# Attention and a mixture of experts on one core: the last attention step reordered, and expert 0's second weights loaded and split later

## The chip, the cores and the metric

The kernel runs on 1 core of one Trainium2 chip. The metric is the device time of one execution in microseconds (us). A core has TensorE (PE, with its weight loads shown as PEld), VectorE (DVE), ScalarE (ACT), GpSimd (POOL) and SyncE (SP, which here only issues loads and stores). Each engine works through its own instructions in order; semaphores tie the engines together.

## The reference

Inputs are q, k, v of shape 8 x 8 x 576 x 64 (batch, head, token, width), a gain vector g, and the experts' weights: a gate 512 x 8, a local gate 512 x 1, w1 8 x 512 x 1024 and w2 8 x 1024 x 512, all float32.

```python
kv = einsum('bhsd,bhse->bhde', k, v)
x = einsum('bhsd,bhde->bhse', q, kv)
x = x / sqrt(mean(x * x, -1) + 1e-6) * g
...
logits = x @ w_gate
local = sigmoid(x @ w_local)
...
e = argmax(logits) if s == 0 or local < 0.5 else previous e
out = softmax(logits)[e] * (relu(x @ w1[e]) @ w2[e])
```

Heads are laid side by side, so x is 8 x 576 x 512 for the second half. Each token goes to one expert; which one depends, where the local gate is high, on the token before it in its batch.

## The kernel before, in words

**Attention in 16 steps.** The batches are taken in four groups of two, and each group in four steps of two heads: step i is group i // 4, head pair i % 4 (`NST` = 16). For a step, SyncE loads six tiles of 288 KB: kt and vt of two batches (`load_kv`, two steps ahead of their product) and qt of two batches (`load_q`). TensorE makes k times v (`kv`, L375), turns kv and multiplies it with the gate for the logits (`turn_kv` L409, `logits_of` L425), turns q (`turn_q` L439 and, for its last columns, `turn_last` L417), and multiplies q with kv in two parts (`q_kv`, L460). GpSimd copies kv into the block-diagonal tile kvz (`kvb_of`, L399), ScalarE copies the logits' columns beside it (L429) and the results out of PSUM into raw (L464). Squares are taken on GpSimd or ScalarE (`squares`, L495 and L493) and summed on VectorE (`sums`, L500).

**Order by letters.** For PE, ACT, DVE and POOL the program's order is the engine's order (`manual_schedule`). In the loop over i, each letter of `STEP` (or of `LATE[i]` for the last steps) calls one branch of `work_of` (L859). Those of interest here: `Q`, `c`/`R` and `a` are q times kv of step i (products of the first part; products and copy of the second part; copy of the first part). `0` and `1` are the two kv copies of step i+1 on GpSimd. `T` and `U` are the turns of q of step i+1, `L` and `l` the logits of step i+1 and their copy into kvz. `m`, `p`, `q`, `b` push on the routing of an earlier group (`SLOTS`, `adv`). `G` closes the pool of kt and vt and issues two gathers on GpSimd (L770), the rows of the first two blocks of 128 tokens of expert 0 (xa). `2` and `3` scale such a block on VectorE (L808) and copy its gate on GpSimd (L928); `4` and `5` turn it on TensorE (L820), cast it on ScalarE (L824) and subtract on VectorE (L825). `o` stores up to three chunks of finished rows to DRAM and, in the steps of `LOADED`, loads one weight piece; `e` loads q of step i+3.

**Weights.** An expert has eight pieces of 512 KB: 0 to 3 of w1, 4 to 7 of w2. `wload` loads a piece into one of four buffers (wst). `wsplit` makes two float32r tiles of it: hi is a copy on ScalarE (L230 or L233), lo the subtraction wst - hi (L231 or L234), by default on VectorE. In the loop `w` is the copy and `v` the subtraction, in the steps of `SPLIT`. Expert 0's piece 7 is split behind the loop, with its subtraction on GpSimd (L1136). Every load and store of SyncE goes through `fetch` (L184), one queue in program order; up to the last step each waits for the landing of the sixth one before it (`LANES`).

**Routing.** `rows_out` (norms, logits, keys) and `route` (each token's place in its expert's list) are generators, pushed on by `adv`. In `route` VectorE builds one-hot tiles co, ab and lo (L710, L717, L740: place columns and lanes compared with a counter, 16-bit results), and TensorE multiplies lo with ab (L723), nine small products, whose sums are the lists of tokens.

**The first expert.** `first_wide` computes relu(w1 x) of the first two blocks, in four pairs of 128 of the 1024 hidden columns (24 products of 256 columns each, L961, L966, L967); behind each pair ScalarE and VectorE make hh and hl (L1031, L1032), and hooks run: a0, a2, a4, a6 of `PASS`. In a hook, `2` and `3` push on the routing of the current group by two or three stages, `o` stores, `s` takes the last step's sums and starts the last group. At a0 to a4 that is the routing of the third group, whose products L723 are in a4 on TensorE, ahead of the fourth pair. Then `second` multiplies with w2 for the first block (hooks b) and the second (hooks c), and scatters the rows from GpSimd (L997); the third and fourth blocks and the other seven experts follow.

Of the kernel before, what the change touches and what calls it, by code (L numbers as in the profile page):

```python
# [22 lines left out]
def kernel(  # L23
# [12 lines left out]
    nc = tc.nc  # L36
# [10 lines left out]
    W = C // 2  # L47
# [7 lines left out]
    NST = NGRP * NP  # L55
# [137 lines left out]
    NW1 = ND  # L193
# [6 lines left out]
    def wload(e, i):  # L200
        t = wpools["w"].tile([P, 2 * DM], F32, name="wst", bufs=4)
        wfetch(t, by[e], i, e > 1)
        staged[e, i] = t
# [36 lines left out]
    def wsplit(e, i, two=False):  # L240
        t = staged.pop((e, i))

        if i < NW1:
            slot = (e * NW1 + i) % (2 * NW1)
            nm, pool = f"w1_{slot}", "s" if slot < NW1 else "b"
        else:
            slot = (e * NW2 + i - NW1) % (NW2 + 2)
            nm, pool = f"w2_{slot}", "scc"[slot] if slot < 3 else "d" if slot < NW2 else "b"
        hi, lo = (wtile(pool, nm + x) for x in "hl")
        low_ = split_w(hi, lo, t, i, e > 1)  # L250
        wt[e, i] = (hi, lo)

        def low(engine=nc.vector):
            low_(engine)
            if to_load:
                wload(*to_load.pop(0))

        if two:
            return low
        low()  # L260
# [214 lines left out]
    def adv(g, n=1):  # L475

        for _ in range(n):
            while next(bg[g][0], "end") == "end":
                bg[g].pop(0)
                if not bg[g]:  # L480
                    return
# [355 lines left out]
        bg[g] = [rows_out(g, raws.pop(g), mss.pop(g), kk), route(g, kk)]  # L837


    LOADED = {i: j for j, i in enumerate((0, 1, 2, 3, 5, 10, 13, 14))}  # L840
    SPLIT = {i: j for j, i in enumerate((2, 4, 6, 8, 11, 12, 15))}

    STEP = "Q0saKcwkopRTq1vLlYVmUxeb"
    LATE = {NST - 3: "QKsw1vqkcabLRpo0mlGTVYXUe", NST - 2: "QcmKkLpTRoUea20qlV13xbsy", NST - 1: "45sQRwvacOyX"}

    SLOTS = {}
    for g in range(NGRP - 1):
# [11 lines left out]
    def work_of(i, what):  # L859


        new, nxt, now = i + 2 < NST, 0 <= i + 1 < NST, i >= 0
        if what in "pmqb":
            for g in SLOTS.get((i, what), ()):
                adv(g)
        elif what == "s" and i > 0:
            for x in range(2):
                sums(i - 1, x)
            if i % NP == 0:
                group(i // NP - 1)  # L870
        elif what == "Q" and now:
            step["a"], step["c"] = q_kv(i)
            next(step["a"])
        elif what == "R" and now:
            next(step["c"])
        elif what in "ac" and now:
            next(step[what])
            done.add((i, what))
        elif what == "K" and new:
            step["k"] = kv(i + 2)  # L880
            next(step["k"])
            for b in range(2):
                load_kv(i + 2 + LB, b)
        elif what == "k" and new:
            next(step["k"])
        elif what == "L" and nxt:
            step["l"] = logits_of(i + 1)
            next(step["l"])
        elif what == "l" and nxt:
            next(step["l"])  # L890
        elif what in "01" and nxt:
            kvb_of(i + 1, int(what))
        elif what == "T" and nxt:
            for b in range(2):
                turn_q(i + 1, b)
        elif what == "U" and nxt:
            turn_last(i + 1)
        elif what == "e" and nxt:
            assert i + 1 in qls and i + 1 in qTs
            for b in range(2):  # L900
                load_q(i + 1 + LQ, b)
        elif what == "V" and new:
            turn_kv(i + 2)
        elif what == "w" and i in SPLIT:
            step["v"] = wsplit(0, SPLIT[i], True)
        elif what == "v" and i in SPLIT:
            step.pop("v")()
        elif what in "xy" and now:
            squares(i, "xy".index(what))
        elif what in "XY" and now:  # L910
            squares(i, "XY".index(what), True)
        elif what == "o":
            store(3)
            if i in LOADED:
                wload(0, LOADED[i])
        elif what == "O":
            store()
        elif what == "G":
            right.close()
            xa = right.enter_context(tc.tile_pool(name="xa", bufs=1, side="right",  # L920
                                                  reuse_waits="tile"))
            xrs.extend(gather(xa.tile([P, NP * PW], F32, name=f"xa{x}"), ahead[x][0], NT - 4 * S)
                       for x in range(2))
        elif what in "23":
            x = int(what) - 2
            scale(xrs[x])
            done.add(what)
            nc.gpsimd.tensor_copy(pe0[:, x:x + 1], gate(xrs[x], 0))  # L928
        elif what in "45":
            x = int(what) - 4  # L930
            assert str(x + 2) in done
            turn(xrs[x], xh, xl, x * P, ps_q, "pq")
# [3 lines left out]
    for i in range(-2, NST):  # L936
        if i == NST - 1:
            paced.clear()
        if i == NST - 2:
            xb = rw.tile([P, C, NP * PW], F32R, name="raw", bufs=3).rearrange("p c w -> p (c w)")  # L940
            xh, xl = (xb[:, o:o + ND * 2 * P].rearrange("p (d t) -> p d t", d=ND)
                      for o in (0, ND * 2 * P))
        for what in LATE.get(i, STEP):
            work_of(i, what)
# [188 lines left out]

    pe3 = const.tile([P, 1], F32, name="pe3")

    wsplit(0, 7, True)(nc.gpsimd)  # L1136


    PASS = dict(at.split(":") for at in "a0:22o2 a2:s a4:223 a6:3 b1:33t b3:o c3:3x c4:3 c6:T3 d0:3z d5:3 d6:3f d7:r3 d11:3 d15:yF3l".split())

    def at(k):

        def do():
            for what in PASS[k]:
                if what == "s":
                    for x in range(2):
                        sums(NST - 1, x)
                    group(G)
                elif what in "23":
                    adv(int(what))  # L1150
                elif what == "t":
                    third_in()
                elif what == "x":
                    third_x()
                elif what == "T":
                    turn(*third, 0, ps_t)
                    done.add("T")
                elif what == "f":
                    fourth_in()
                elif what == "o":  # L1160
                    store()
                elif what == "r":
                    ranks()
                    read_ranks()
                elif what == "z":
                    sel_in()
                elif what == "l":
                    limits()
                elif what == "y":
                    scale(fourth[0])  # L1170
                    done.add("y")
                elif what == "F":
                    assert "y" in done
                    turn(*fourth, 0, ps_t)
                    done.add("F")
        return do if k in PASS else None

    def places(k, n):
        return [(f, at(f"{k}{f}")) for f in range(n) if f"{k}{f}" in PASS]

# [284 lines left out]
```

## Time and the profile before

| what | us |
|---|---|
| median of 3 runs | 585.01 |
| lowest and highest of these | 582.82, 588.82 |
| the profiled execution | 578.19 |
| its span, first to last instruction | 576.4 |
| TensorE busy in the span | 550.8 |
| VectorE, ScalarE, GpSimd busy | 303.4, 245.3, 239.3 |

The profile is of one execution. Times in it are microseconds from the start of the span, mean times of one instruction nanoseconds. A line L460 is line 460 of the kernel; "out<-in" names the tiles an instruction writes and reads. "a <- b" in a wait means that the engine sat idle until b. "issue" is time for which the profile shows no cause. PEclk is TensorE's granted clock as a share of full speed; DMA is the mean busy share of the core's 16 DMA engines.

### The profile page before, as it was taken

How to read it: one execution, taken by the hardware profiler on the slowest of the kernel's cores; microseconds unless marked ns; L12 is line 12 of the kernel's file. 1: busy time of each engine (PE TensorE's matmuls, PEld its weight loads, DVE VectorE, ACT ScalarE, POOL GpSimd, SP SyncE). 2: the span in 40 equal slices, each digit the busy share in tenths (PEclk: the TensorE clock that was granted, in tenths of full speed). 3: DMA queues.
4: the chain of work that ended last, by engine and by line, in shares of the span. 5: the costliest groups of instructions: out<-in, count | busy, mean ns of one | idle time of the engine just before them, and what ended most of it. 6: DMA issues, size and time to landing. Idle time of an engine off the chain costs nothing.

```text
span 576.4 us, 11828 instructions
## 1 busy us (share of the span) xinstructions
PE 550.8 (96%) x4645; PEld 488.9 (85%) x4645; DVE 303.4 (53%) x627; ACT 245.3 (43%) x451; POOL 239.3 (42%) x305
## 2 busy tenths in 40 slices
PE   2999998879999999999999999999999999999996
PEld 2888887769878989898999898989698979899895
DVE  1125786769686525635463745463646545664510
ACT  1578887762254333332434334333433343435220
POOL 5234433251245527334353762467145734542001
PEclk9999999989999999999999999999999999999999
DMA  7999999970666454233343452346234533432000
GB/s 232 318 349 358 335 346 356 319 268 22 239 234 236 125 178 133 68 107 101 121 115 121 132 141 82 124 142 172 65 119 154 149 105 127 141 106 80 18 19 30
DMA packets 41376, 94.91 MB, mean 165 GB/s; under 512 B 7263, under 2 KB 7263, under 8 KB 41312
## 3 DMA queue, kind: packets, MB, share of 16 engines
q1 hardware_dynamic: 32032, 72.64, 36.9%
q0 software_dynamic: 7744, 21.41, 12.7%
q8 instruction: 38, 0.62, 0.5%
q10 hardware_dynamic: 1536, 0.02, 0.1%
q14 instruction: 26, 0.21, 0.1%
HBM read 73.85 MB, written 20.86 MB: 164 GB/s over the span
## 4 chain that ended last, share of the span: by engine, by line
PE 82%; DMA 9%; issue 3%; ACT 3%; DVE 2%; POOLq 0%; POOL 0%; SPq 0%; DVEq 0%; ACTq 0%
PE ph L966 12%; PE ph L961 12%; PE ph L967 12%; PE py L961 11%; PE py L967 11%; PE py L966 11%; PE po L460 5%; DMA qt<-in_q_dram 4%; PE po L375 2%; ACT qT L440 1%; PE pq L439 1%; PE py L1011 1%; DMA xs<-raw 1%; DMA vt<-in_v_dram 1%; PE pt L820 1%
## 5 line engine op out<-in xcount | busy, mean ns | idle before, releaser
L780 POOL DMA_INDIRECT xr<-xs,gid x120 | 136.5, 1137 | 36.6 <-issue 34.2
L1032 DVE SCALAR_TENSOR_TENSOR hl<-ph,hh 128x384 fp32r<-128x384 f32 (+3 forms) x92 | 52.3, 569 | 125.9 <-ACT hh L1031 105.3
L997 POOL DMA_INDIRECT out_dram<-ot,sidr x34 | 34.8, 1025 | 172.3 <-ACT ot L996 130.2
L1031 ACT ACTIVATE hh<-ph 128x384 fp32r<-128x384 f32 (+3 forms) x92 | 46.7, 510 | 132.7 <-PE ph L967 99.1
L996 ACT ACTIVATE ot<-py,pe 128x512 f32<-128x512 f32 (+1 forms) x37 | 25.5, 688 | 59.0 <-PE py L967 36.0
L460 PE MATMUL po<-kvz,qT 128*64 128x146 f32 x512 | 43.7, 298 | 0.5 <-ACT kvz L429 0.4
L495 POOL TENSOR_TENSOR sq<-raw 128x576 f32<-128x576 f32 x16 | 20.4, 1275 | 53.6 <-ACT raw L464 42.8
L460 PEld LDWEIGHTS po<-kvz,qT 128*64 128x64 f32 x512 | 33.8, 139 | 6.3 <-POOL kvz L399 1.9
L500 DVE TENSOR_REDUCE ms<-sq 128x9 f32<-128x576 f32 x32 | 23.1, 749 | 23.0 <-POOL sq L495 21.2
L375 PE MATMUL po<-vt,kt 64*64 64x64 f32 x1152 | 23.2, 232 | 11.0 <-DMA vt<-in_v_dram 11.0
L375 PEld LDWEIGHTS po<-vt,kt 64*64 64x64 f32 x1152 | 20.7, 145 | 14.5 <-issue 9.6
L464 ACT COPY raw<-po 128x876 f32<-128x876 f32 (+1 forms) x32 | 22.8, 715 | 11.6 <-PE po L460 11.3
L399 POOL COPY kvz<-kvp 64x128 f32<-64x128 f32 x64 | 20.1, 314 | 13.9 <-ACT kvp L379 9.0
L808 DVE TENSOR_TENSOR xr<-xr 128x512 f32<-128x512 f32 x37 | 25.5, 688 | 0.0
L801 ACT CAST yh<-xT 128x512 fp32r<-128x512 f32 x17 | 10.5, 620 | 31.4 <-DVE xT L797 27.3
L961 PE MATMUL py<-w_1h,hh 128*128 128x512 f32 (+1 forms) x56 | 22.2, 396 | 0.0
L967 PE MATMUL py<-w_0h,hl 128*128 128x512 f32 (+1 forms) x56 | 22.0, 393 | 0.1
L961 PE MATMUL py<-w_0h,hh 128*128 128x512 f32 (+1 forms) x56 | 21.9, 392 | 0.0
L966 PE MATMUL py<-w_0l,hh 128*128 128x512 f32 (+1 forms) x56 | 21.9, 391 | 0.0
L967 PE MATMUL py<-w_1h,hl 128*128 128x512 f32 (+1 forms) x56 | 21.9, 390 | 0.0
L966 PE MATMUL py<-w_1l,hh 128*128 128x512 f32 (+1 forms) x56 | 21.8, 390 | 0.0
L797 DVE STREAM_TRANSPOSE xT<-xr 128x512 f32<-128x512 f32 x30 | 21.2, 706 | 0.4
(433 smaller groups left out, 1651.7 us busy)
## 6 DMA issues: line engine op xcount, KB each, us to landing
wst<-in_moe_w_dram SPq DMA_DIRECT2D x64, 512.0 KB
xs<-raw SPq DMA_DIRECT2D x36, 292.0 KB
kt<-in_k_dram SPq DMA_DIRECT2D x32, 288.0 KB
vt<-in_v_dram SPq DMA_DIRECT2D x32, 288.0 KB
qt<-in_q_dram SPq DMA_DIRECT2D x32, 288.0 KB
xr<-xs,gid POOLq DMA_INDIRECT x120
out_dram<-ot,sidr POOLq DMA_INDIRECT x36
xr<-xs,gidr POOLq DMA_INDIRECT x6
```

Source lines behind the costliest of these rows:

```text
L375: nc.tensor.matmul(pk[half(x ^ b), x, 0:D], ks[b][half(x), cd], vs[b][half(x), cd], start=(c == 0), stop=(c == C - 1))
L460: nc.tensor.matmul(po[half(b), x, o:o + n], lw[:, half(x)], kvb[:, z0:z0 + n], start=True, stop=True)
L500: nc.vector.tensor_reduce(mss[g][:, :, 2 * n + x], sqs.pop((s, x)), axis=AX.X, op=ALU.add)
L780: i = nc.gpsimd.indirect_dma_start(out=xr[:, u * PW:(u + 1) * PW], out_offset=None, in_=xs.rearrange("t (q w) -> (t q) w", w=PW), in_offse ...
L808: (engine or nc.vector).tensor_mul(xv, xv, r.unsqueeze(3).to_broadcast([P, NP, 2, D]))
L961: mm = nc.tensor.matmul(ps, ah, bh, start=(first and i == 0), stop=False)
L966: nc.tensor.matmul(ps, ah, bl, start=False, stop=False)
L967: nc.tensor.matmul(ps, al, bh, start=False, stop=(last and i == n - 1))
L996: nc.scalar.activation(ot[0:m], po[0:m], AF.Copy, scale=pe[0:m])
L997: return nc.gpsimd.indirect_dma_start(out=outf, out_offset=bass.IndirectOffsetOnAxis(ap=idx[0:m], axis=0), in_=ot[0:m], in_offset=None, bo ...
L1031: nc.scalar.activation(hh, ps, AF.Relu)
L1032: nc.vector.scalar_tensor_tensor(hl, ps[:, :, 0:nl], 0.0, hh[:, :, 0:nl].bitcast(F32), op0=ALU.max, op1=ALU.subtract)
```

## The change

Loads: pieces 4 to 7 of expert 0 are no longer loaded in steps 5, 10, 13 and 14, but by a new letter `W`, two in step 12 behind its last letter (so behind the last q load, which is `e` of step 12), two in step 13. Splits: pieces 4 and 5 are no longer split in steps 11 and 12 nor 6 in step 15; piece 4 is split in step 15, and 5, 6 and 7 in the hooks a0, a2 and a4, copied on ScalarE and subtracted on GpSimd. Order: the gathers `G` move from step 13 to step 14, behind the kv copies `0` and `1`, which now come first in that step; `T` stands ahead of `L` there, and `2` and `3` at the end; in step 15 q times kv (`Q`, `R`, `a`, `c`) stands ahead of the turns `4` and `5`, and the sums `s` first.

```diff
-    LOADED = {i: j for j, i in enumerate((0, 1, 2, 3, 5, 10, 13, 14))}
-    SPLIT = {i: j for j, i in enumerate((2, 4, 6, 8, 11, 12, 15))}
+    LOADED = {i: j for j, i in enumerate((0, 1, 2, 3))}
+    SPLIT = {i: j for j, i in enumerate((2, 4, 6, 8, 15))}
 
     STEP = "Q0saKcwkopRTq1vLlYVmUxeb"
-    LATE = {NST - 3: "QKsw1vqkcabLRpo0mlGTVYXUe", NST - 2: "QcmKkLpTRoUea20qlV13xbsy", NST - 1: "45sQRwvacOyX"}
+    LATE = {NST - 4: STEP + "W", NST - 3: "QKsw1vqkcabLRpWo0mlTVYXUe",
+            NST - 2: "01GQcmTLpURoeaqlXbs2y3", NST - 1: "sQRac45wvOyX"}
...
+        elif what == "W":
+            for j in range(2):
+                wload(0, NW1 + 2 * (i - NST + 4) + j)
...
-    wsplit(0, 7, True)(nc.gpsimd)
-
-
-    PASS = dict(at.split(":") for at in "a0:22o2 a2:s a4:223 a6:3 b1:33t b3:o c3:3x c4:3 c6:T3 d0:3z d5:3 d6:3f d7:r3 d11:3 d15:yF3l".split())
+    PASS = dict(at.split(":") for at in "a0:522o2 a2:6s a4:7223 a6:3 b1:33t b3:o c3:3x c4:3 c6:T3 d0:3z d5:3 d6:3f d7:r3 d11:3 d15:yF3l".split())
...
+                elif what in "567":
+                    wsplit(0, int(what), True)(nc.gpsimd)
```

## Rows read from the trace of the kernel before

**Rows 1.** Page, part 2: TensorE's busy tenths in 40 slices of 14.4 us.

```profile
PE   2999998879999999999999999999999999999996
```

**Rows 2.** Chain of waits, 109 to 125 us: start, us, what.

```profile
109.55 4.14 DMA qt<-in_q_dram
113.72 1.23 POOL xa L770
...
115.26 4.82 DMA xa<-xs,gi
120.10 0.70 DVE xa L808
120.89 1.09 PE pt L820 x4
121.98 3.42 PE po L460 x40
```

**Rows 3.** Windows: busy us (x count) of PE, PEld, DVE, ACT, POOL; PEclk; DMA share; GB/s.

```profile
98.00:112.00 14.00, 12.49 (x264) 10.40 (x261) 11.17 (x25) 9.42 (x26) 2.59 (x6) 1.00 0.99 336
...
116.40:120.60 4.20, 1.32 (x9) 0.64 (x7) 2.33 (x7) 3.71 (x10) 0.80 (x3) 1.00 0.90 290
120.60:124.10 3.50, 3.21 (x22) 2.84 (x24) 3.39 (x6) 1.53 (x2) 3.32 (x6) 0.51 1.02 382
...
125.40:137.90 12.50, 12.50 (x119) 12.42 (x119) 9.09 (x26) 4.66 (x9) 3.93 (x3) 1.00 0.15 53
```

**Rows 4.** Timeline of SyncE, weight loads of steps 5 and 10.

```profile
56.86 0.39 SPq L186 DMA_DIRECT2D wst<-in_moe_w_dram  x1
...
94.37 0.71 SPq L186 DMA_DIRECT2D wst<-in_moe_w_dram  x1
```

**Rows 5.** Waits of SyncE, 54 to 62: us in total, times, longest.

```profile
SPq L186 <- PE po L375: 2.3, 2, 1.2
```

**Rows 6.** Timeline, PE, ACT and DVE, 112 to 124: start, us, engine, line, operation.

```profile
112.28 2.26 PE L460 MATMUL po<-kvz,qT 128*64 128x146 f32 x31
...
114.38 0.53 PE L460 MATMUL po<-kvz,ql 128*64 128x73 f32 x7
...
115.62 1.04 PE L439 MATMUL pq<-ident,qt 128*128 128x128 f32 x8
...
119.11 0.74 ACT L429 COPY kvz<-pm 64x18 f32<-64x18 f32 x4
...
122.03 1.30 DVE L825 TENSOR_TENSOR raw<-pt,raw 128x512 fp32r<-128x512 f32 x2
```

**Rows 7.** Timeline, POOL and DVE, 61 to 88.

```profile
62.25 1.76 POOL L495 TENSOR_TENSOR sq<-raw 128x576 f32<-128x576 f32 x1 [3.44 <-ACT raw L464]
...
61.73 1.27 DVE L234 SCALAR_TENSOR_TENSOR w_2l<-wst,gcol,w_2h 128x1024 fp32r<-128x1024 f32 x1
62.92 1.19 DVE L664 TENSOR_TENSOR mks<-kk,m 128x81 f32<-128x81 f32 x1
...
87.35 0.24 DVE L664 TENSOR_TENSOR mks<-kk,m 128x81 f32<-128x81 f32 x1
```

**Rows 8.** Timeline, ACT, POOL, DVE and PE, 126 to 135.

```profile
126.66 1.03 ACT L230 CAST w_3h<-wst 128x1024 fp32r<-128x1024 f32 x1
128.45 0.60 ACT L1031 ACTIVATE hh<-ph 128x512 fp32r<-128x512 f32 x1 [0.76 <-PE ph L967]
...
127.76 2.39 POOL L231 TENSOR_TENSOR w_3l<-wst,w_3h 128x1024 fp32r<-128x1024 f32 x1 [0.52 <-ACT w_3h L230]
...
130.20 0.17 DVE L698 TENSOR_SCALAR col<-place 128x9 int32<-128x9 int32 x1
...
132.23 1.35 DVE L740 TENSOR_TENSOR lo<-lane,iota_l 128x1152 bf16<-128x1152 int32 x1
...
134.57 0.56 PE L723 MATMUL rbank<-ab,lo 128*128 128x96 bf16 x9
```

## The prediction

> **What bounds the kernel now.** I read four views in this order. First the page's slices: TensorE is full in nearly every slice [rows 1], so from the first expert's products to the end each microsecond of the end is a microsecond of TensorE, and only a place where TensorE waits can give anything back. Second the chain of waits, to find those places. There is one cluster, where the sixteen attention steps hand over to the experts [rows 2]: the last q load lands at 113.7, GpSimd's first gather of token rows starts on it, the second gather lands at 120.1, its scaling and turning take until 122.0, the last step's q times kv until 125.4, and there expert 0's first product starts. Third the windows [rows 3]: between 116.4 and 120.6 TensorE works 1.32 of 4.20 us, and in the 3.5 us behind that its granted clock is 0.51, the lower of the two levels; from 125.4 to 137.9 it works all 12.50 us at full clock. Fourth SyncE's issues and the engines' timelines, for what would move.
>
> So the sum has two terms: how much earlier than 125.4 the first product starts, and whether the 12.5 us behind it stay free of waits, since the change puts three subtractions on GpSimd there.
>
> **Loads taken from the front.** Eight weight loads of 0.524 MB belong to expert 0. Two of the second weights are issued at 56.86 and 94.37 [rows 4], between the q, k and v loads; the change puts them behind the last q. At 336 GB/s [rows 3] each took 0.524 MB / 336 GB/s = 1.56 us of transfer time. Behind the second the DMA share is 0.99 and the chain ends on a q load [rows 2, 3], so I count it whole. The first stood where SyncE still waited for TensorE to release kv buffers, 2.3 us in 8 [rows 5], so the loop was then paced by TensorE and part of the load was hidden: between 0 and 1.56, I take 0.9, the middle rounded up because the queue stays full from there on. Sum 2.4 us, bounds 1.5 and 3.1. ScalarE and VectorE also lose a copy and a subtraction each in steps 11 and 12; they are off the path, I count nothing (if they were on it, this adds to the gain).
>
> **The new order of the tail.** Today the q of step 15 is turned at 115.62, and its logits are in kvz at 119.11 + 0.74 = 119.85, 4.2 us later [rows 6]. In the new order the turn comes directly behind step 14's q times kv, which ends at 114.38 + 0.53 = 114.91; less 2.4 that is 112.5. I add 0.6 to the 4.2, a choice, because the product for the logits and the route's product now stand between the turn of q and the turn of its last columns: 117.3. Then q times kv, 112.28 to 114.91 in step 14, so 2.6: 119.9. Then both turns of gathered rows, 1.1 [rows 2]: 121.0. What hid their copies and subtractions before (q times kv) now stands ahead of them, so the first product waits: from 121.98, where the turns end now, to 122.03 + 1.30 = 123.33 is 1.35. The first product would start at 122.4.
>
> The other branch is the gather. The kv copies of step 15 go ahead of it on GpSimd, and they need nothing late. It starts 2.4 earlier, at 111.3; from its start to the second gather's start is 1.54, to its landing 4.82 [rows 2]: 117.7; scale 0.70 and the two subtractions 1.30: 119.7. The two sums that now stand ahead of the subtractions on VectorE would need 2.7 us to make this branch the later one. But four weight loads, 2.1 MB and 6.2 us at 336 GB/s, are now in flight beside both gathers where there was one. If they got half their number ahead of the second gather it would be 3.1 later and the start 122.8, so the branch is close; I leave the start at 122.4 and put 1.0 into the range. The clock was at its lower level in the last steps [rows 3]; new gaps (about 2.4 us before q times kv, 1.35 before the first product) may bring it again, up to 1.7 us lost in 3.5 us at 0.51, or save the loss that is paid today. I take no difference.
>
> Term one: 125.4 - 122.4 = 3.0, I take 2.8 earlier (bounds 0.5 and 4.2).
>
> **Three subtractions on GpSimd.** Pieces 5, 6 and 7 of expert 0's second weights are now copied on ScalarE and subtracted on GpSimd behind the first, second and third pair of blocks of the first product (a0, a2, a4). One takes 2.39 us there [rows 8]. As work this fits: GpSimd is busy 3.93 of the 12.5 us [rows 3], and alone, the three would be done about 7.1, 10.6 and 13.7 us after the start (worked out below), while the second product, which starts 12.5 behind it, takes its pieces in order and comes to piece 7 last.
>
> What it does to VectorE is another matter. At 62.25 GpSimd starts squares while VectorE is in a subtraction with two inputs from SBUF (61.73 to 63.00); they take 1.76, and VectorE's next small product, with two such inputs, takes 1.19, where the same instruction takes 0.24 at 87.35 with GpSimd idle [rows 7]. The two engines took turns, each for a whole instruction. Now lay GpSimd's subtractions over the stretch. ScalarE's relu of the first pair ends at 129.05, 3.65 behind the start; the copy behind it takes 1.03; so the first subtraction runs from about 4.7 to 7.1. VectorE has at that time the routing of the third group: from 130.20 (4.8 behind the start) to 132.23 + 1.35 = 133.58 it makes the one-hot tiles, 3.4 us, nearly all of it in instructions with two SBUF inputs [rows 8]. They wait until 7.1. Between 7.8 and 8.2 the second piece is copied (four pairs in 12.5 us, so 3.1 apart, and the route's small products behind the first), VectorE is then in the middle of its 3.4 us, and GpSimd gets the next turn. With that turn VectorE's chain ends at 7.1 + 3.4 + 2.39 = 12.9. TensorE has nine small products on that tile in its order at 134.57, 9.2 behind the start, ahead of the fourth pair, and waits: 12.9 - 9.2 = 3.7 us. Bounds: 0, if these instructions don't exclude each other; 1.3, if only the first subtraction gets in the way (7.1 + 3.4 - 9.2); 6.1, if the third, ready some 3.1 behind the second, also goes ahead of the last VectorE one (another 2.39). I take 3.7, the value of taking turns, which is what the rows show.
>
> The Trainium skill, "SBUF — State Buffer", section "Who interferes with whom", states the same as an exclusive lock on a port pair shared by the two engines, held for a whole instruction, and names a VectorE instruction with two SBUF inputs against a GpSimd instruction that reads SBUF. The trace agrees for 32-bit tiles (1.19 against 0.24); no row of before shows the 16-bit ones of the routing beside GpSimd, and the rule includes them: with it the sum is the one above, without it the first rival's.
>
> **The sum.** 2.8 earlier, 3.7 waited: 0.9 us later. The profiled execution took 578.2 (its span 576.4), so 579.1. The three runs have a median of 585.0, 6.8 above the profiled one, and spread over 6 us; on that scale the forecast is 585.9. A measurement of this kernel tells about 1% (5.9 us) from no change, so this is "within 1%".
>
> **Rivals.** (1) *No wait at the one-hot tiles*: the 16-bit instructions are not held up, or GpSimd comes late enough. For it: GpSimd's 2.39 us one at 127.76 held nothing up in the trace; against: VectorE was then waiting or on one-SBUF-input work. Only term one is left: 582.2. (2) *The wait is the long one*, the slower side: the third subtraction also goes first, TensorE waits 6.1, and the idle time drops its clock as it did at 120.6, 1.7 more: 7.8 - 2.8 = 5.0 later, 590.0. It decides as soon as the wait at the one-hot tiles is over 2.8. Against it: the rows show turns, not two GpSimd instructions in a row. (3) *The loads were hidden anyway*: the loop is paced by TensorE, or the gathers queue behind the four loads; term one shrinks to 0.5, the wait stays: 3.2 later, 588.2. For it rows 5, against it the chain through q loads.
>
> **How the numbers follow.** Forecast 0.46, rival 1 0.28, rival 2 0.12, rival 3 0.10, the rest 0.04. The likeliest has its own range of 583 to 589 (term one's bounds). With rival 1 below and half of rival 2 above, and some 2.5 us for medians of three runs, 579.5 to 591.0 holds 8 in 10. Faster by over 1% (under 579.2) needs rival 1 at its best: 0.08. Slower by over 1% (over 590.9) needs rival 2 or 3 at the bad end: 0.12. Within 1%: 0.80.
>
> **What would show it.** Right: no weight load between q loads; the first product near 122.4; some of VectorE's routing instructions stretched to over 2 us beside a 2.39 us GpSimd subtraction; TensorE idle 3 to 4 us ahead of the nine small products (L723 before). Wrong: the last of them at 1.35, ending before TensorE comes to it (rival 1); a first product at 125 (rival 3). A wait of the second product for piece 6 or 7 would be a cost that I priced at nothing.

## The result, and the profile after

The changed kernel takes 590.74 us (median of 20 runs, 585.95 to 600.24), the kernel before 585.18 us beside it (20 runs, 575.92 to 590.57). The ratio is 1.0145, with a 95% interval of 1.0108 to 1.0181: slower by some 8.5 us, where 0.9 us was forecast. The ratio leaves out each run more than 1.5% above its kernel's shortest, which is taken to be in a slower state of the chip, and so goes by 8 of the 20 runs before and 16 of the 20 after; the medians of all runs lie 5.6 us (0.95%) apart. The profiled executions are 578.19 us before and 585.95 us after, 7.8 us apart, with spans of 576.4 and 584.1 us, so the two traces carry a difference of that size.

The page's slices after, TensorE's busy tenths and its granted clock. A slice is now 14.6 us. The dent of [rows 1], 8, 8, 7 in the 7th to the 9th slice, is 8, 7, 7 in the 8th to the 10th (131 to 146 us), and the 13th slice, 175 to 190 us, is an 8:

```profile
PE   2999999877998999999999999999999999999996
...
PEclk9999999988999999999999999999999999999999
```

The windows after, columns as in [rows 3]:

```profile
116.40:120.60 4.20, 2.19 (x17) 1.73 (x17) 2.67 (x14) 3.26 (x10) 0.00 (x0) 0.81 1.01 381
120.60:124.10 3.50, 3.50 (x39) 3.21 (x36) 3.47 (x5) 1.95 (x3) 2.22 (x3) 0.74 1.04 387
126.64:140.00 13.36, 10.18 (x94) 9.94 (x95) 10.55 (x13) 4.92 (x7) 7.57 (x3) 0.98 0.04 12
...
139.20:144.04 4.84, 4.82 (x34) 4.83 (x34) 4.63 (x16) 0.62 (x2) 3.25 (x2) 0.65 0.00 0
```

In the 13.4 us behind the first product TensorE works 10.2 us; before, it worked all of the 12.5 us to the second product. GpSimd has 7.57 us of work there (before 3.93), and from 139.20 to the second product at 144.04 TensorE's granted clock is 0.65.

The timeline after, by engine (start, us, engine, line, what; in brackets the idle time before it and what ended it). First the hand-over to the first product:

```profile
108.38 1.52 SPq L186 DMA_DIRECT2D qt<-in_q_dram  x2
109.95 2.76 SPq L186 DMA_DIRECT2D wst<-in_moe_w_dram  x4
...
113.44 1.24 POOL L770 DMA_INDIRECT xa<-xs,gi  x1 [2.67 <-DMA qt<-in_q_dram]
120.80 0.18 POOL L932 COPY pe<-xa 128x1 f32<-128x1 f32 x1 [4.80 <-DMA xa<-xs,gi]
...
117.68 0.23 DVE L548 TENSOR_REDUCE se<-pe 128x9 f32<-128x72 f32 x1 [5.06 <-ACT pe L546]
121.83 2.24 DVE L808 TENSOR_TENSOR xa<-xa 128x512 f32<-128x512 f32 x2
125.31 1.27 DVE L825 TENSOR_TENSOR raw<-pt,raw 128x512 fp32r<-128x512 f32 x2
...
115.31 1.09 PE L439 MATMUL pq<-ident,qt 128*128 128x128 f32 x8
119.50 3.67 PE L460 MATMUL po<-kvz,qT 128*64 128x146 f32 x31 [2.01 <-ACT kvz L429]
...
123.48 1.32 PE L820 MATMUL pt<-ident,xa 128*128 128x128 f32 x8
126.64 0.39 PE L965 MATMUL ph<-raw,w_0h 128*128 128x256 f32 x1 [1.84 <-DVE raw L825]
...
131.37 2.41 POOL L231 TENSOR_TENSOR w_1l<-wst,w_1h 128x1024 fp32r<-128x1024 f32 x1 [5.34 <-ACT w_1h L230]
134.84 3.11 POOL L231 TENSOR_TENSOR w_2l<-wst,w_2h 128x1024 fp32r<-128x1024 f32 x1 [1.07 <-ACT w_2h L230]
137.90 3.49 POOL L231 TENSOR_TENSOR w_3l<-wst,w_3h 128x1024 fp32r<-128x1024 f32 x1
...
131.51 2.29 DVE L698 TENSOR_SCALAR col<-place 128x9 int32<-128x9 int32 x1
134.68 1.06 DVE L717 TENSOR_TENSOR ab<-co,idab 128x864 bf16<-128x864 bf16 x1
135.66 3.50 DVE L740 TENSOR_TENSOR lo<-lane,iota_l 128x1152 bf16<-128x1152 int32 x1
...
139.22 0.68 PE L723 MATMUL rbank<-ab,lo 128*128 128x96 bf16 x9 [3.18 <-DVE lo L740]
144.04 0.39 PE L965 MATMUL py<-w_0h,hh 128*128 128x512 f32 x1
```

The rows of before that these are read against, and one window of it (columns as in [rows 3]):

```profile
108.84 1.50 SPq L186 DMA_DIRECT2D qt<-in_q_dram  x2
117.53 0.18 POOL L928 COPY pe<-xa 128x1 f32<-128x1 f32 x1 [1.26 <-DMA xa<-xs,gi]
121.91 3.23 PE L460 MATMUL po<-kvz,qT 128*64 128x146 f32 x32
125.33 0.39 PE L961 MATMUL ph<-raw,w_0h 128*128 128x256 f32 x1
137.85 0.40 PE L961 MATMUL py<-w_0h,hh 128*128 128x512 f32 x1
...
134.57:137.85 3.28, 3.28 (x35) 3.28 (x34) 3.07 (x14) 1.22 (x3) 0.34 (x1) 1.00 0.00 0
```

Four stretches are to be seen. *The loads*: all four stand behind the last q, but the gather starts only 0.3 us earlier than before (113.44 against 113.72 in [rows 2]), and its rows land 7.4 us later (120.80); in the trace of before the same copy stands at 117.53, 3.8 us behind. *The order*: q times kv waits 2.0 us for the logits in kvz and runs 3.67 us where step 14's took 2.26 in [rows 6] (the clock of 120.6 to 124.1 is 0.74; step 15's own took 3.23 before, with 0.51 in that window [rows 3]); then the turns' subtractions, which ended under q times kv in [rows 6], hold the first product 1.8 us. It starts at 126.64 instead of 125.4. *The collision*: L698 takes 2.29 us instead of 0.17 and L740 3.50 instead of 1.35 [rows 8]; the nine small products stand 12.58 us behind the first product, where they stood 9.2 behind it. *Behind it*: the second product starts 17.40 us behind the first, instead of 12.5.

The waits of TensorE after, from 84 to 160 us (engine, line, what it waited for: us, times, longest):

```profile
PE rbank L723 <- DVE lo L740: 3.2, 1, 3.2
PE po L460 <- ACT kvz L429: 2.4, 2, 2.0
PE ph L965 <- DVE raw L825: 1.8, 1, 1.8
PE pm L425 <- issue: 1.0, 1, 1.0
```

So of the 7.7 us between the spans, 1.3 lie ahead of the first product (126.64 - 125.33), 4.9 between the first and the second (17.40 - 12.52), and 1.5 behind that, in small waits (the longest, 0.9 us, for the scaling of a block of gathered rows, lies in the slice from 175 us).

### The profile page after: what moved, and what is told of

The parts are those of the page before. It is cut to its first block, busy times and chain, and to the rows that moved or that the text cites. A ratio compares the mean times of both kernels' runs of the same rounds, so it can differ in the third digit from the quotient of the medians.

```text
span 584.1 us, 11831 instructions
## 1 busy us (share of the span) xinstructions
PE 553.2 (95%) x4645; PEld 491.4 (84%) x4645; DVE 304.8 (52%) x625; ACT 245.9 (42%) x452; POOL 244.1 (42%) x306
## 4 chain that ended last, share of the span: by engine, by line
PE 82%; DMA 7%; issue 3%; ACT 3%; DVE 3%; another core or an unknown queue 1%; POOLq 0%; SPq 0%; POOL 0%; DVEq 0%; ACTq 0%
PE ph L971 11%; PE ph L965 11%; PE ph L970 11%; PE py L971 11%; PE py L965 11%; PE py L970 11%; PE po L460 7%; PE po L375 3%; PE pq L439 2%; ACT qT L440 2%; DMA qt<-in_q_dram 2%; DMA xr<-xs,gidr 1%; PE py L1015 1%; DMA kt<-in_k_dram 1%; DMA vt<-in_v_dram 1%
## 5 line engine op out<-in xcount | busy, mean ns | idle before, releaser
L375 PE MATMUL po<-vt,kt 64*64 64x64 f32 x1152 | 23.5, 233 | 11.3 <-DMA vt<-in_v_dram 11.3
L399 POOL COPY kvz<-kvp 64x128 f32<-64x128 f32 x64 | 18.8, 293 | 16.1 <-ACT kvp L379 9.3
```

Source lines behind the costliest of these rows:

```text
L375: nc.tensor.matmul(pk[half(x ^ b), x, 0:D], ks[b][half(x), cd], vs[b][half(x), cd], start=(c == 0), stop=(c == C - 1))
```

## The experiments

Ratios are to the kernel before, timed on the same chip beside it, with 95% intervals. Each diff is against the kernel that its sentence names; "first to second" is the time from the first to the second product in the run's profile (12.5 before, 17.4 after).

**The collision.** `dve_subs` is the changed kernel with the three subtractions on VectorE:

```diff
-                    wsplit(0, int(what), True)(nc.gpsimd)
+                    wsplit(0, int(what), True)(nc.vector)
```

> The changed kernel with one edit: the subtractions of pieces 5, 6 and 7 in a0, a2 and a4 on VectorE (1.22 us each there) instead of GpSimd. If the two engines hold each other up (theory 1), VectorE's col and lo instructions are back at 0.17 and 1.35 us (2.29 and 3.50 in the changed kernel), TensorE's wait of 3.4 us ahead of the nine products L723 falls under 1, no lower clock follows it, and the kernel is some 4 to 5 us faster than the changed one: ratio to before near 1.006. If VectorE's chain is simply too long there or the loss sits in the last attention steps (theory 2), the wait stays near 3 or the time stays at a ratio of 1.012 to 1.017.

Measured 1.0054 (1.0018 to 1.0089): 0.9% of the 1.45% goes, some 5 us. L698 is back at 0.17 us, L740 at 1.35, and the wait of L723 is gone. The lower clock is not: its profile, of one of the longest runs of its set (590.04 us), has 15.47 us from first to second, with a granted clock of 0.80 in them.

`subs_halved` is the changed kernel with each GpSimd subtraction issued as two of half the columns (512):

```diff
-            return lambda engine: engine.tensor_sub(lo, t, hi.bitcast(F32))
+            def low(engine):
+                for x in range(2 if engine is nc.gpsimd else 1):
+                    c = slice(x * DM, (x + 1) * DM) if engine is nc.gpsimd else slice(0, 2 * DM)
+                    engine.tensor_sub(lo[:, c], t[:, c], hi[:, c].bitcast(F32))
+            return low
```

> The changed kernel with each of GpSimd's three subtractions made as two of 512 columns (about 1.2 us each instead of 2.4). If the two engines hold each other up a whole instruction at a time, VectorE's col instruction is stretched to about 1.2 us instead of 2.29 and the next ones wait again for the second halves; GpSimd's sum of work ahead of lo is about the same, so TensorE's wait at L723 stays between 2 and 4 us and the ratio between 1.010 and 1.016. If the engines shared the access evenly, halving would change none of VectorE's durations.

Measured 1.0086 (1.0052 to 1.012), below the range expected. Its timeline of VectorE and GpSimd (lines are 4 further on), and from its waits the one of the small products:

```profile
131.02 1.18 DVE L702 TENSOR_SCALAR col<-place 128x9 int32<-128x9 int32 x1
132.44 1.45 DVE L714 TENSOR_TENSOR co<-col,ccode 128x432 bf16<-128x432 int32 x1
134.90 2.43 DVE L744 TENSOR_TENSOR lo<-lane,iota_l 128x1152 bf16<-128x1152 int32 x1
...
134.35 4.12 POOL L234 TENSOR_TENSOR w_2l<-wst,w_2h 128x512 fp32r<-128x512 f32 x2 [0.93 <-ACT w_2h L230]
...
PE rbank L727 <- DVE lo L744: 1.8, 1, 1.8
```

Each hold-up is now about 1.1 us (2.43 - 1.35, 1.18 - 0.17), half of the 2.15 of the whole instruction, and there are more of them: the engines take turns by the instruction. The wait falls from 3.2 to 1.8 us, also below what was expected.

`subs_moved` keeps the subtractions on GpSimd but puts them where VectorE makes no one-hot tiles, and puts the routing's letter `p` ahead of `T` in step 14:

```diff
-            NST - 2: "01GQcmTLpURoeaqlXbs2y3", NST - 1: "sQRac45wvOyX"}
+            NST - 2: "01GQcmLpTURoeaqlXbs2y3", NST - 1: "sQRac45wvOyX"}
...
+    wsplit(0, 5, True)(nc.gpsimd)
...
-a0:522o2 a2:6s a4:7223 a6:3
+a0:22o2 a2:s a4:2236 a6:37
```

> The changed kernel with p ahead of T, and GpSimd's three subtractions kept on GpSimd but moved out of VectorE's routing: piece 5 ahead of the first product, 6 behind the nine products in a4, 7 in a6. Theory 1: the wait at L723 is under 1 us although GpSimd does the same work, and the ratio is near that of the run with both repairs (1.000 to 1.003). If GpSimd's speed itself were the trouble, the second product would wait for piece 6 or 7 instead, 1 to 3 us, and the ratio stays near 1.007 or above.

Measured 1.005 (1.0022 to 1.0078), first to second 13.3 us, no wait at L723: as good as on VectorE (`dve_route` below, 1.0055), though above the 1.003 expected. It is the meeting that costs, not GpSimd's work. Its pair with the same letters is `route_first` (below, 1.0096), and that pair, like `route_first` and `dve_route`, prices the collision at 0.4 to 0.5%; after and `dve_subs`, and `loads_only` and `loads_dve` (below), price it at 0.9%. With intervals of 0.3 to 0.4% to either side, 0.4 to 0.9% is what the runs tell.

**The order.** `order_only` is the kernel before with the new letters of steps 13 to 15 and its own loads and splits; `turns_only` has only the new step 15; `kv_only` has the kv copies ahead of the gathers, both in step 14, with the old step 15:

```diff
     order_only
+    NST - 3: "QKsw1vqkcabLRpo0mlTVYXUe", NST - 2: "01GQcmTLpURoeaqlXbs2y3", NST - 1: "sQRac45wvOyX"
     turns_only
+    NST - 3: "QKsw1vqkcabLRpo0mlGTVYXUe", NST - 2: "QcmKkLpTRoUea20qlV13xbsy", NST - 1: "sQRac45wvOyX"
     kv_only
+    NST - 3: "QKsw1vqkcabLRpo0mlTVYXUe", NST - 2: "01GQcmLpTRoUea2qlV3xbsy", NST - 1: "45sQRwvacOyX"
```

> The kernel before with the new order of steps 13 to 15 alone; loads and splits as before. Theory 1: no wait at L723, since only piece 7 is subtracted on GpSimd and ahead of that stretch; what is left is the handover, which in the changed kernel's profile had TensorE's lower clock in q times kv and the first product 1.2 us later, so a ratio between 0.998 and 1.005. Theory 2 (the order is the loss): a ratio near 1.012.

> The kernel before with step 15's new order alone: q times kv ahead of the turns of the gathered rows; the gathers and the kv copies stay where they were. If the turns' place is what the order costs, the ratio is 1.004 or more (the kv copies still stand behind the gathers on GpSimd, so q times kv is no earlier, and the turns with 1.8 us of cast and subtraction come behind it: 2 to 4 us). If it is the gathers' place, within 0.002 of 1.0.

> The kernel before with the kv copies of the last step ahead of the gathers, and both in step 14, but the turns ahead of q times kv as they were. If the turns' place is what the new order costs, the ratio is 0.998 to 1.001 here; if the gathers' place in step 14 is, 1.003 to 1.005, with a first gather that starts later behind the same last q.

Measured 1.0048 (1.0013 to 1.0082), 1.0063 (1.0033 to 1.0092) and 0.9994 (0.9967 to 1.0021). The place of the gathers costs nothing that these runs tell; the new step 15, with the turns behind q times kv, costs half a per cent. The timeline of `turns_only`:

```profile
121.32 3.93 PE L460 MATMUL po<-kvz,qT 128*64 128x146 f32 x31 [1.86 <-ACT kvz L429]
125.56 1.09 PE L820 MATMUL pt<-ident,xa 128*128 128x128 f32 x8
127.38 0.38 PE L961 MATMUL ph<-raw,w_0h 128*128 128x256 f32 x1 [0.73 <-ACT raw L824]
```

With the turns behind it, q times kv has nothing ahead of it to cover the wait for kvz (1.9 to 2.0 us in every kernel with the new step 15, none in the others), and leaves the cast and the subtraction of the turned rows uncovered. With the turns ahead of it each covers the other. From the start of the turn of q to the first product the kernels with the new step 15 take 8.3 to 11.3 us; those with the old one take 6.3 to 6.5 us where TensorE waits under 0.7 us for gathered rows (`kv_only`, `late_67`, `front_clear`, `repaired_dve`), and up to 12.9 us (`loads_dve`) where it waits longer. The clock does not go with the order: q times kv takes 3.93 us here but 2.42 in `order_only`, and in the old order between 2.2 (`kv_only`) and 4.1 us (`loads_only`).

`route_first` is the changed kernel with only `p` ahead of `T`, `order_route` is `order_only` with that, `dve_route` is `dve_subs` with that:

```diff
-            NST - 2: "01GQcmTLpURoeaqlXbs2y3"
+            NST - 2: "01GQcmLpTURoeaqlXbs2y3"
```

> The changed kernel with p (the routing's exp on ScalarE, and all of VectorE's routing behind it) ahead of T (turns of q and their copies) in step 14, as it was before. In the changed kernel VectorE waits 5.06 us for that exp at 112.6, and its whole queue follows 3 to 4 us later, down to the subtractions of the turned rows that release the first product. If that is the loss of the handover, the 5 us wait is gone, the first product starts 1 to 2 us earlier against q times kv, and the ratio falls from 1.0145 to 1.011; if the copies of the logits and the clock set it, nothing changes. The wait at L723 stays at 3 us or more either way.

> The kernel before with the new order of steps 13 to 15, but p ahead of T; loads and splits as before. If the order's 0.5% came from ScalarE's exp standing behind the copies of q's turn, the ratio is 1.000 or a little less; if it came from the turns standing behind q times kv (their cast and subtraction, 1.8 us of wait ahead of the first product), it stays near 1.004.

> The changed kernel with both repairs: subtractions on VectorE, and p ahead of T in step 14. If the two losses are separate (0.009 and 0.005), the ratio is 1.0005, that is no difference from before; if they overlap, 1.004 or more. Routing instructions at 0.17 and 1.35 us, the first product some 1 us earlier than in the changed kernel, counted from the start of step 14's q times kv.

Measured 1.0096 (1.0054 to 1.0138), 1.004 (1.0013 to 1.0068) and 1.0055 (1.0026 to 1.0085). VectorE's wait of 5.06 us for the routing's exponential halves, the first product comes 1.0 to 1.6 us earlier behind the turn of q, but beside `order_only` and `dve_subs` no time follows that a measurement tells; `dve_route` misses its expectation. `route_first` is 0.5% below the changed kernel, with intervals that overlap. So the wait of VectorE is not shown to be the order's loss.

**The loads.** `loads_only` has the loads and GpSimd splits of the change with the old order; `loads_dve` is that with VectorE's subtractions; `late_67` is `loads_dve` with pieces 6 and 7 loaded in step 14, behind its stores; `late_67_order` is `subs_moved` with that place of the loads:

```diff
     loads_only, loads_dve
+    NST - 4: STEP + "W", NST - 3: "QKsw1vqkcabLRpWo0mlGTVYXUe", NST - 2: "QcmKkLpTRoUea20qlV13xbsy", NST - 1: "45sQRwvacOyX"
     late_67
+    NST - 4: STEP + "W", NST - 3: "QKsw1vqkcabLRpo0mlGTVYXUe", NST - 2: "QcmKkLpTRoWUea20qlV13xbsy", NST - 1: "45sQRwvacOyX"
```

> The changed kernel with the order of steps 14 and 15, and the gathers' place, as in the kernel before; weight loads behind the last q and three subtractions on GpSimd stay. Theory 1: VectorE's routing instructions are stretched to over 2 us, TensorE waits 3 us or more at L723, ratio 1.006 to 1.012; nearer 1.005 if the loads taken from the front save their 2.4 us, nearer 1.012 if the loop hid them. Theory 2: a ratio within 0.003 of 1.0 or below it.

> The changed kernel with the order of steps 13 to 15 as before and the subtractions of pieces 5, 6 and 7 on VectorE: the later loads and splits alone, without GpSimd's part. If the loads taken from the front save time at all, the ratio to before is under 0.999 (my forecast's 2.4 us would be 0.996). If the loop hid them and the four loads only crowd the last steps, 1.000 to 1.006. Theory 1 wants it some 0.009 below the run with the three subtractions on GpSimd (1.0121): 1.003.

> The run with the later loads and VectorE's subtractions in the old order (1.0034), but pieces 6 and 7 loaded in step 14 behind its three stores instead of in step 13, so that only two loads stand beside the gathers. If four loads in flight are what makes the first gather take 7.0 us to its landing (3.8 before), it takes under 5.5 here, and the ratio falls to 1.000 or below (0.998 if the front of the loop gains too). If the gathers don't care, 1.003 again.

> The run with the new order, p ahead of T, and GpSimd's subtractions moved out of VectorE's routing (1.005), with pieces 6 and 7 behind step 14's stores as well. In this order the gathers are not what the first product waits for, so if the loss of 0.005 is the order's own (cast and subtraction of the turned rows uncovered, lower clock at the first product) it stays between 1.003 and 1.006; if the crowded gathers are the loss, it falls to 1.000 or below.

Measured 1.0121 (1.0079 to 1.0163), 1.0034 (1.0008 to 1.006), 1.0009 (0.9983 to 1.0034) and 1.0051 (1.0029 to 1.0074). The waits of TensorE in `loads_dve`, 112 to 160 us, and the gather in its timeline:

```profile
PE pt L820 <- DVE xa L808: 4.9, 1, 4.9
...
114.84 1.23 POOL L770 DMA_INDIRECT xa<-xs,gi  x1 [8.52 <-DMA qt<-in_q_dram]
...
121.87 0.71 POOL L932 COPY pe<-xa 128x1 f32<-128x1 f32 x1 [4.49 <-DMA xa<-xs,gi]
```

The turns wait 4.9 us for the gathered rows, which come 7.0 us behind the gather's start. In `late_67`, with two loads beside the gather, the copy stands 4.3 us behind it (119.46 - 115.18) and that wait is gone. The ratios go the same way, with intervals that overlap. The old order shows the crowded gather in the open; the new one hides it behind q times kv and pays with the two waits above: no wait for gathered rows is among the rows of after, and `late_67_order`, with two loads away from the gathers, is where `subs_moved` was (1.0051 and 1.005). Nor do the later loads show their gain in the new order: `order_only` has the old loads and 1.0048, `dve_subs` the new ones and 1.0054, timed side by side.

`no_loads` is the kernel before in which pieces 4 and 5 are never loaded:

```diff
+            if LOADED.get(i) in (4, 5):
+                t = wpools["w"].tile([P, 2 * DM], F32, name="wst", bufs=4)
+                nc.gpsimd.memset(t, 0.0)
+                staged[0, LOADED[i]] = t
...
```

> The kernel before, but pieces 4 and 5 of expert 0's second weights are never loaded: GpSimd fills their buffers with zeros instead, so 1.05 MB is gone from the transfers and expert 0's second product uses zeros for half of its weights. It sizes what taking these two loads from between the q, k and v loads can give at most. If the transfers pace the loop there (my forecast's 2.4 us), the ratio is 0.994 to 0.997 and the gather starts 2 to 3 us earlier against the first product of the loop; if the loop is paced by TensorE and the loads were hidden, 0.998 to 1.001.

Measured 0.9951 (0.9925 to 0.9977), about 2.8 us: leaving the two front loads out gives what the prediction took for moving them, or a little more.

`front_clear` takes all four out of the way in the old order (4 and 5 in steps 13 and 14; 6 and 7 by a letter `Z` in step 15 behind its stores; 5 split on GpSimd ahead of the first product, 6 and 7 on VectorE at a2 and a4):

```diff
-    LOADED = {i: j for j, i in enumerate((0, 1, 2, 3))}
+    LOADED = {i: j for j, i in enumerate((0, 1, 2, 3, 13, 14))}
...
+NST - 3: "QKsw1vqkcabLRpo0mlGTVYXUe", NST - 2: "QcmKkLpTRoUea20qlV13xbsy", NST - 1: "45sQRwvacOZyX"
...
```

> The kernel before, in its old order, with pieces 4 to 7 out of the q, k and v loads and away from the gathers: 4 in step 13 and 5 in step 14 (where 6 and 7 were), 6 and 7 in step 15 behind the stores; 4 split in step 15, 5 on GpSimd ahead of the first product, 6 and 7 on VectorE in a2 and a4, behind its routing. If the front's gain is the 0.5% of the run without these loads and only crowding and GpSimd gave it back, the ratio is 0.994 to 0.997; if the gain cannot be kept (second product waiting for piece 6 or 7, or stores late), 0.998 to 1.003.

Measured 1.0019 (0.9988 to 1.005): a miss. Its profiled run had the first product at 121.05 us and a span of 570.9, but the runs' medians are 576.36 and 576.95, so that one profile does not stand for them.

**All three undone.** `repaired` is the changed kernel with the old step 15, the loads of `late_67` and the subtractions of `subs_moved`; `repaired_z` loads 6 and 7 only in step 15; `repaired_dve` is `repaired` with the subtractions on VectorE, in the hooks of the change:

```diff
     repaired, repaired_dve
+    NST - 4: STEP + "W", NST - 3: "QKsw1vqkcabLRpo0mlTVYXUe", NST - 2: "01GQcmLpTRoWUea2qlV3xbsy", NST - 1: "45sQRwvacOyX"
     repaired_z
+    NST - 2: "01GQcmLpTRoUea2qlV3xbsy", NST - 1: "45sQRwvacOWyX"
```

> The changed kernel with its three suspected costs undone at once: the turns of the gathered rows again ahead of q times kv in step 15 (the kv copies stay ahead of the gathers), pieces 6 and 7 loaded in step 14 behind the stores instead of beside the gathers, and the GpSimd subtractions of 5, 6 and 7 put where VectorE has no one-hot tiles (5 ahead of the first product, 6 behind the nine small products, 7 behind the last pair). If the costs are these three and nothing else (collision about 0.9%, order 0.4 to 0.6%, crowded gathers about 0.3%), they add up to the whole 1.45%, and the front loads' gain is about what the later loads still cost: ratio 0.997 to 1.002, second product 12.4 to 13.3 us behind the first. If something else of the change costs, or the three are not additive (the collision's price hides the order's): 1.004 or more.

> As the one before, with pieces 6 and 7 loaded only in step 15, behind its stores, so that no weight load is issued beside the gathers. If the loads behind the gathers are what keeps the front loads' 2.8 us from showing, 0.994 to 0.998 and the second gather lands under 4.5 us after its start. If the late loads themselves become late (the second product waiting for piece 6 or 7, or the route's gathers crowded instead), 1.000 or more with that wait in the profile.

> As the run with the three costs undone, but with the subtractions of pieces 5, 6 and 7 on VectorE (behind the first, second and third pair) instead of moved ones on GpSimd. If what is left there is the GpSimd subtractions at their new places, or the spread of that set of runs, this one comes out at 0.997 to 1.002, as the two halves of it did alone (0.9994 for the kv copies first, 1.0009 for the later loads); the second product 12.4 to 13.3 us behind the first. If the kv copies first and the later loads together cost something that neither costs alone: 1.004 to 1.008, with a wait at the turns of the gathered rows longer than the 1.7 us there.

Measured 1.0071 (1.0017 to 1.0125), 1.0111 (1.0023 to 1.0198) and 0.9952 (0.9916 to 0.9988). By these ratios the first two miss. But they set all 12 and all 6 of their runs against the 6 shortest of 17 runs of before, because one of those, at 574.03 us, is 4.8 us below the next; the medians of all runs are 583.14 and 584.28 beside 583.45 us, 0.9995 and 1.0014. So no loss of `repaired` is shown, and by its median it meets its expectation. The third comes out a little faster than before, by more than it was expected to; the medians of all its runs, 582.99 and 584.48 us, give 0.9975, which lies within the expectation. The waits of TensorE in `repaired_dve`, 112 to 160 us, and VectorE's scaling in its timeline:

```profile
PE rbank L683 <- DVE oh L674: 1.0, 1, 1.0
PE pt L820 <- ACT ql L419: 0.7, 1, 0.7
PE pl L417 <- ACT qT L440: 0.4, 2, 0.2
PE rbank L723 <- DVE lo L740: 0.4, 1, 0.4
...
120.47 1.43 DVE L808 TENSOR_TENSOR xa<-xa 128x512 f32<-128x512 f32 x2
```

None of the three large waits is left: these rows make 2.5 us, the three large ones of after 7.0 (3.2, 2.0 and 1.8). Its first product stands 6.3 us behind the start of the turn of step 15's q (125.12 - 118.81; before 125.33 - 115.62 = 9.7). The runs of before in these last two sets spread over 12 to 17 us, and `repaired_dve` was timed in one set only, so the sign of its gain is surer than its size.

`repaired` and `repaired_dve` differ only in the subtractions, and those of `repaired` still meet VectorE: moved away from the one-hot tiles, they stand beside the norms of the last group. A line of VectorE in `repaired`, the same line in `repaired_dve`, and a wait of TensorE in `repaired`:

```profile
134.36 2.41 DVE L512 SCALAR_TENSOR_TENSOR t<-t,a 128x72 f32<-128x72 f32 x1
...
140.83 0.23 DVE L512 SCALAR_TENSOR_TENSOR t<-t,a 128x72 f32<-128x72 f32 x1
...
PE py L971 <- DVE hl L1036: 1.2, 1, 1.2
```

TensorE waits 1.2 us there in the second product (0.9 in `subs_moved`, 1.2 in `late_67_order`); no such wait stands in `repaired_dve`. The profile of `repaired` is of a run of 587.77 us, 4.6 above its median; its span behind the second product is 451.3 us instead of 438.5. Over all the profiles that span lies between 435.9 and 451.3 us, though no edit touches the other experts' products, so it says nothing of the edit.

## Why the prediction was wrong

**The step that failed is term one**, "2.8 earlier". In the profile the first product came 1.3 us later than before. In the timed runs `dve_subs`, the changed kernel without the collision, is 0.5% (3 us) slower than before, where term one alone would have made it 2.8 us faster. The sum had the first product at 122.4 and it came at 126.64; of these 4.2 us, 2.8 lie in where the new chain starts and 1.4 in the chain.

*The start: the loads taken from the front gave nothing.* The sum turns the q of step 15 at 112.5; it was turned at 115.31, hardly earlier than before (115.62). The last q is issued only 0.5 us earlier (108.38, before 108.84), and how much of that is the spread between executions one profile can't say. "2.4 us, bounds 1.5 and 3.1" is the right size for leaving the loads out (2.8 us in `no_loads`), but moved they are still transferred, and no place tried for them shows the gain: `dve_subs` beside `order_only`, and in the old order `loads_dve` (1.0034), `late_67` (1.0009) and `front_clear` (1.0019). In the old order a part of it goes to the crowded gathers: their rows come 7.0 us behind the first gather's start instead of 3.8, and TensorE waits 4.9 us. The prediction saw this ("if they got half their number ahead of the second gather it would be 3.1 later") and left that branch at 119.7. In the changed kernel the rows come as late (7.4 us) but nothing waits for them; why the gain fails to come there stays open.

*The chain: the order was taken as free, in truth it costs.* From the turn of q to the first product the sum has 9.9 us, the profile 11.3: 4.2 to the start of q times kv (4.8 in the sum), 4.0 for it, to the turns at 123.48 (2.6), and 3.2 for the turns and the wait behind them (2.5). The pieces were nearly right; what it missed is that in the old order the turns of gathered rows fill the wait for kvz, and q times kv covers the subtractions. `order_only` shows 0.5% for the whole order, `turns_only` 0.6% for step 15 alone, `kv_only` nothing for the kv copies and the gathers. The 9.7 us of the profile of before hide this, for its second gather came late and its clock was low: `kv_only`, as fast in the timed runs, needs 6.5.

*The clock: "I take no difference."* The 2.6 us are step 14's q times kv, at full clock. Step 15's ran at a lower clock before (3.23 us) and does so after (3.67), so the sum counted as saved a loss that this profile still pays.

**Three subtractions on GpSimd: right in mechanism and nearly in size.** Forecast 3.7 us at L723, taking turns; measured 3.2 (3.34 by the position, 12.58 - 9.24). All the signs it named for them are there: the first subtraction holds L698, GpSimd gets the second turn ahead of L740, the third comes too late to add. What was short is the price behind the wait: from the nine small products to the second product TensorE takes 4.82 us at a granted clock of 0.65, where it took 3.28 at full clock before. That is 1.5 us, and 3.34 + 1.54 is the 4.9 found between the two products. The prediction had such a loss (1.7 us) only in its second rival. The timed pairs price the whole at 0.4 to 0.9%, 2 to 5 us.

The Trainium skill, "SBUF — State Buffer", section "Who interferes with whom", has this as a lock held for a whole instruction, decided by who issues first. The trace agrees for the 16-bit results (L740, 1.35 to 3.50) and by the halves (1.1 instead of 2.15).

**The rivals.** Rival 1 (no wait at the one-hot tiles) is refuted. Rival 2 was closest to the time, by the wrong wait: not three subtractions in a row, but two turns and the clock. Rival 3's second half, gathers behind the four loads, happened; its first, that the loads were hidden, did not (0.9951 in `no_loads`), but moved they gave no more than if they had been.

**The sum by parts**: collision 0.4 to 0.9%, order 0.4 to 0.6%, the later loads nothing either way in the new order (crowded gathers some 0.2 to 0.3% in the old one). That makes 0.8 to 1.5%; measured are 1.45% by the ratio and 0.95% by the medians of all runs. `repaired_dve` and, by its median, `repaired` have the three undone, as far as that goes, and are not slower than before, which supports the sum. That the parts add up to the measured loss is likely and not shown.

**Left open**: why no place of the loads shows the gain of `no_loads` (`front_clear`, `late_67`, `repaired_z`); the waits of 0.3 to 2.6 us named "issue" ahead of L425 and L409; and whether the gain of `repaired_dve` holds in a second set.

## What to carry to other kernels

Before work goes to GpSimd, look at what VectorE does in the same stretch: while one engine's instruction with SBUF inputs runs, an instruction of the other can stand for its whole length, and a TensorE product behind it pays with the wait and the clock. A load moved off a critical transfer is still transferred: look for what is then in flight beside it, and do not take the gain of leaving it out for the gain of moving it. And when two pieces of work cover each other's waits, swapping them opens both, though neither has become longer.

## What the runs showed of the hardware

- The hold-up by GpSimd's subtraction also met an instruction with a single small SBUF input and a 9-element row: L698, 0.17 to 2.29 us, and 1.18 beside halved subtractions. The prediction counted on tiles with two inputs.
- A gather of 128 rows lands 3.8 to 4.7 us behind its start beside one weight load of 512 KB (3.8 before, 4.7 in `turns_only`), 3.9 to 5.3 beside two (`late_67_order`, `repaired`) and 6.4 to 7.4 beside four (`subs_halved`, `dve_route`), by the first instruction that uses its rows.
- VectorE's L512, 72 elements a row with two SBUF inputs, took 2.41 us beside a GpSimd subtraction in `repaired`, 0.23 in `repaired_dve`.
- The last q is issued at 105.94 in `subs_halved`, 108.38 after and 110.02 in `dve_subs`, three kernels that are the same program up to there. So a term of 1 to 3 us needs timed runs, not one profile.
